# Hedgehog attention and a squared-ReLU FFN on one core: 24 output stores issued from GpSimd's queue in place of SyncE's

## The chip, the core and the metric

The kernel runs on one core of a Trainium2 chip. A core has a matrix engine (TensorE, PE in the profile), a vector engine (VectorE, DVE), a scalar engine (ScalarE, ACT), a general engine (GpSimd, POOL) and a synchronization engine (SyncE, SP), which here only issues DMAs. Each engine runs its own stream of instructions in order; they meet at semaphores. DMAs are issued by SP, ACT and POOL, and 16 DMA engines move the bytes. The metric is device time in microseconds (us); less is better.

## The reference

```python
def phi(x):
    proj = np.einsum('bhsd,df->bhsf', x, w_phi)
    proj = proj - np.max(np.abs(proj), axis=-1, keepdims=True)
    return np.concatenate([np.exp(proj), np.exp(-proj)], axis=-1)
q_p, k_p = (phi(q), phi(k))
kv = np.einsum('bhsf,bhsd->bhfd', k_p, v)
z = np.sum(k_p, axis=2)
num = np.einsum('bhsf,bhfd->bhsd', q_p, kv)
den = np.einsum('bhsf,bhf->bhs', q_p, z)[..., None] + 1e-06
attn = num / den
x = attn.transpose(0, 2, 1, 3).reshape(B * S, H * D)
h = np.maximum(x @ w_in, 0.0)
out = h * h @ w_out
```

Sizes: 8 batches, 8 heads, 576 tokens, head size 64, 128 features (256 with both signs); then 4608 tokens of 512 values through a layer of 2048. Inputs and the output are 32-bit floats in the chip's main memory (HBM). The kernel computes in bf16 with sums in 32 bits.

## The kernel before

**Attention.** For each batch the kernel loads k, q and v (L249, L257, L269; batch 0 and 1 also L278) with DMAs issued by GpSimd, which turn the floats into bf16 on the way. There are two buffers for each of k, q and v (`xk`, `xq`, `xv`), so batch b + 2 goes where batch b was. From batch 2 on, k and q are turned by DMA transposes issued by SP into `kT` and `qT` (L331); TensorE projects them with `w_phi` (L347), VectorE takes the maxima of their absolute values (L405, L498, L531), and ScalarE makes the exponentials. `va` (L428) is v, scaled; TensorE sums k's features times `va` into `kv` (L462). For batches 3 to 7 q's features are made with tokens in the partitions (`qf`, L544) and turned by another DMA transpose on SP into `qpn` (L548). TensorE then multiplies `qpn` with `kv` (L648), VectorE divides (L660 to L674) into `xo`, and a third kind of DMA transpose on SP (L708) turns `xo` into `xT`, which the FFN takes. The last 64 tokens of each batch are gathered in `xS`.

**FFN.** Its tokens come in 9 chunks of 512: chunk c is the first 512 tokens of batch c, and chunk 8 is all that is gathered in `xS`. The first product is `ffn_in` (L788, 64 matmuls of 512 columns a chunk); ScalarE or VectorE takes the ReLU out of PSUM into `hr` (L765, L767), VectorE squares it into `h` (L774). The second is `ffn_out` (L882): four output tiles of 128 tokens by 512 values a chunk. ScalarE or VectorE copies each tile out of PSUM to one of four buffers `ot` (`copy`, L193 and L195), and a DMA stores it to `out` (L900; 256 KB). Chunk 8 stores halves (L897), and its last tile pieces of these (L869). An `ot` buffer is written again four tiles later, and its store must have landed by then.

**The order of work.** The function does not emit instructions straight away. It adds operations to a plan (`Plan.add`), and at the end emits them in a written-out list, `ORDER`, of some 1,680 operation numbers; the attention of one batch is thereby laced with the FFN of the batches before. `pin` chains each instruction behind the one that its engine got before, so every engine, and the DMA queue of every engine, goes through its share of `ORDER` in that order. An instruction that waits holds everything behind it on its engine. `BASES` gives the PSUM banks, `STATES` picks ScalarE or VectorE for the copies that either could do, and `GATES` names, for each load of batches 2 to 7, one more operation that it must wait for. These lists are constants. The engine name and the cost that `add` is given matter to whoever made the lists; for an operation without an alternative they change nothing that is emitted. What decides who issues a DMA is the call inside `fn` (`nc.sync` or `nc.gpsimd`).

So SP's queue holds, in order, the transposes of L331, L548 and L708 and the stores of L900 and L897, and POOL's queue holds the loads. A DMA also waits on its queue for the semaphore that it will raise to be free: each kind of queue has eight, used in turn, so a DMA is issued when the one eight before it has landed.

Of the kernel before, what the change touches and what calls it, by code (L numbers as in the profile page):

```python
# [20 lines left out]
def act_cost(n):  # L21
    return max(n / 1200 + 0.050, 0.105), n / 1200 + 0.165 + SEM


def dve_cost(n):
    return n / 960 + 0.064, n / 960 + 0.150 + SEM


def pe_cost(n, each):
    return n * each, n * each + 0.165 + SEM  # L30
# [23 lines left out]
class Plan:  # L54
# [6 lines left out]
    def add(self, eng, cost, fn, r=(), w=(), opens=None, closes=None, dma=None, tiled=False, release=False, what="", lock=None):  # L61
        op = Op(eng, cost, fn, opens, closes, dma, tiled, release, len(self.ops), what)
        op.lock = lock
        before = {}

        def after(o, wait):
            before[o] = max(before.get(o, 0.0), wait)

        for t in r:
            o = self.writer.get(t)  # L70
            if o is not None:
                after(o, 0.0 if o.eng == eng == "PE" else 1.0)
        for t in w:
            o = self.writer.get(t)
            if o is not None:
                after(o, 0.0 if o.eng == eng else 1.0)
            for o in self.readers.get(t, ()):
                after(o, 0.0 if o.eng == eng else 1.0)
        for t in r:
            self.readers.setdefault(t, []).append(op)  # L80
        for t in w:
            self.writer[t] = op
            self.readers[t] = []
        before.pop(op, None)
        for o, wait in before.items():
            o.succ[op] = wait
        op.n = len(before)
        self.ops.append(op)
        self.banks.extend(op.opens)
        return op  # L90
# [18 lines left out]
def kernel(  # L109
# [10 lines left out]
    nc = tc.nc  # L120
# [12 lines left out]
    def dep(i, before, kind):  # L133
        tc.add_manual_dep(i, before, mybir.DependencyInfo(kind, mybir.DependencyReason.DATA), reason="order")

    def pin(ins):
        i = ins.ins
        before = last_on.get(i.engine)
        if before is not None:
            dep(i, before, mybir.DependencyClass.NoSync)  # L140
        last_on[i.engine] = i.name
        if now[0].seq in GATES:
            dep(i, plan.ops[GATES[now[0].seq]].ins, mybir.DependencyClass.Sync)
        now[0].ins = i.name
        return ins
# [8 lines left out]
    def ring(name, n, shape, dt=BF16):  # L154
        return [sb(f"{name}{i}", shape, dt) for i in range(n)]
# [27 lines left out]
    ot = ring("ot", NOT, [DM], F32)  # L183
    SL = (B * S // P - 1) % NOT
# [3 lines left out]
    add = plan.add  # L188

    def copy(out, in_):  # L190

        if now[0].eng == "DVE":
            pin(nc.vector.tensor_copy(out=out, in_=in_))  # L193
        else:
            pin(nc.scalar.activation(out=out, in_=in_, func=ACT.Copy))  # L195

    def ps1(g):
        return psum[:, g.base, :]
# [556 lines left out]
                    out_ops(c)  # L755


    hslot = [0]

    def relu_sq(g, dst, toks):  # L760
# [112 lines left out]
    def ffn_out(c, tt, part):  # L873
        if (c, tt) == (NCH - 1, 3):
            last_out(c, tt, part)
            return
        if part == 0:
            opb[c, tt] = Bank(1, "op")
        g = opb[c, tt]
        def fn():  # L880
            for mc in range(4 * part, 4 * part + 4):
                pin(nc.tensor.matmul(out=ps1(g), lhsT=h2[c % 2][mc // 4][:, mc % 4, tt * P : (tt + 1) * P],  # L882
                                     rhs=wout[mc // 4][:, mc % 4, :], start=(mc == 0), stop=(mc == MC - 1)))
        add("PE", pe_cost(4, 0.216), fn, r=[("wout", part)] + [("h2", c % 2, 4 * part + i, tt) for i in range(4)],
            w=[g], opens=g if part == 0 else None, what="F2")
        if part == 3:
            sl = oslot[0] % NOT
            oslot[0] += 1
            def fn():
                copy(ot[sl], ps1(g))  # L890
            o = add("ACT", act_cost(512), fn, r=[g], w=[("ot", sl)], closes=g, what="ot")
            plan.either((o, "DVE", dve_cost(512)))
            for u in range(2 if c == NCH - 1 else 1):
                def fn(u=u):
                    if c == NCH - 1:
                        b = 2 * tt + u
                        pin(nc.sync.dma_start(out=out[b * S + 512 : b * S + 576, :], in_=ot[sl][u * 64 : u * 64 + 64, :]))  # L897
                    else:
                        o = out[c * S : c * S + 512, :].rearrange("(p j) n -> j p n", j=4)[tt]
                        pin(nc.sync.dma_start(out=o, in_=ot[sl]))  # L900
                add("SP", (0.5, 0), fn, r=[("ot", sl)] + [("ot", SL, half) for half in range(2) if sl == SL],
                    dma=(0.37 if c == NCH - 1 else 0.74, HW_IN, "st"), what="st")


    for hi in range(2):
        def f_kcast(hi=hi):
            copy(xk[0][:, 256 * hi : 256 * hi + 256], ot[2][:, 256 * hi : 256 * hi + 256])
        o = add("DVE", dve_cost(256), f_kcast, r=[("xkf", hi)], w=[("xkh", hi)], what="kcast")
# [21 lines left out]
    for c in range(NCH + 1):  # L930
        if c + 1 < B:
            b = c + 1
            if b >= 2:
                load(k, xk, b, "xk", prs=PIECES, release=True)
                load_q(b, release=True, prs=PIECES)
                load(v, xv, b, "xv", prs=PIECES, release=True)
            attention(b)
        for i in range(16):
            if c == 0:
                if i < 4:  # L940
                    ffn_in_halves(c, 0, i)
                elif i < 8:
                    ffn_in_small(c, 1, i % 4)
                else:
                    ffn_in_pair(c, i - 8)
            elif c < NCH:
                ffn_in(c, i)
            if c >= 1:
                ffn_out(c - 1, i // 4, i % 4)
# [158 lines left out]
```

## Time and profile before

| | |
|---|---|
| median of 3 runs | 344.13 us (344.02 to 344.96) |
| profiled execution, first to last instruction (its span; no other time of it is known) | 344.8 us |
| granted TensorE clock, mean | 0.998 |
| busy: PE, DVE, ACT, POOL | 335.5, 264.2, 225.4, 95.5 us |
| stores of 256 KB by SP | 32, median 2.9 us from issue to landing |
| loads and other DMAs by POOL | 138 instructions |
| moved by DMAs | 51.51 MB, 149 GB/s mean |

A row of the groups reads: line, engine, operation, what it writes and reads, shape, count, then the time that the group was busy, the mean of one, and the engine's idle time just before them with what ended it. PE's busy time counts pipelined matmuls; a matmul of 512 columns shows 0.38 us while four in a row take 0.86 us. The issue of a DMA takes time on the engine's queue (SPq, or POOL itself), its landing comes later. In the timeline rows the first number is the start in us from the start of the span, the second the time that the row covers; several alike are merged with a count (x2). The chain of work that ended last is followed back from the end, and its DMA entries are stretches in which the next step stood waiting for a transfer.

### The profile page before, as it was taken

The page shows a single profiled execution, that of the slowest core. Times are in us where ns is not written, and L with a number is a line of the kernel's source. Part 1 is how long each engine was busy: PE and PEld are TensorE (multiplying, and loading weights), DVE is VectorE, ACT ScalarE, POOL GpSimd, SP SyncE. Part 2 cuts the span into 40 slices and gives each one's busy share as a digit, 9 for nine tenths or more (in the row PEclk, how much of TensorE's full clock was granted, in tenths as well). Part 3 has the DMA queues.
Part 4 walks back from the last instruction along what each step waited for, and adds up shares of the span by engine and source line. Part 5 has one row for each costly group of instructions (what it writes and reads, how often), then busy time and mean ns, then how long its engine had stood idle before and what let it go on. Part 6 is the DMA issues. An engine that isn't in the chain of part 4 may idle for free.

```text
span 344.8 us, 8417 instructions
## 1 busy us (share of the span) xinstructions
PE 335.5 (97%) x3389; PEld 188.3 (55%) x3389; DVE 264.2 (77%) x485; ACT 225.4 (65%) x393; POOL 95.5 (28%) x143
## 2 busy tenths in 40 slices
PE   8999999799999999999999999999999999999995
PEld 7679776444654555545545554565555444444443
DVE  4999999699877987788898999687876635757510
ACT  4999996489898898476887797798475503210031
POOL 8670671681730390104604051240000000000000
PEclk9999999999999999999999999999999999999999
DMA  9999999999999999999999999999864821101024
GB/s 139 179 206 202 199 132 157 153 118 205 170 175 172 227 165 185 195 182 183 171 207 172 199 164 195 188 154 168 196 125 96 157 62 38 63 0 61 32 68 115
DMA packets 142935, 51.51 MB, mean 149 GB/s; under 512 B 111472, under 2 KB 138416, under 8 KB 142896
## 3 DMA queue, kind: packets, MB, share of 16 engines
q1 hardware_dynamic: 97488, 32.35, 50.7%
q0 software_dynamic: 44960, 18.23, 46.7%
q8 instruction: 26, 0.43, 0.5%
q10 hardware_dynamic: 448, 0.39, 0.4%
q14 instruction: 13, 0.11, 0.1%
HBM read 36.73 MB, written 9.44 MB: 134 GB/s over the span
## 4 chain that ended last, share of the span: by engine, by line
PE 87%; DMA 6%; DVE 3%; ACT 1%; POOL 1%; issue 0%; POOLq 0%; DVEq 0%; SPq 0%
PE psum L788 32%; PE psum L882 31%; PE psum L648 5%; PE psum L462 5%; PE psum L347 5%; DMA xT<-xo 4%; DMA qpn<-qf 3%; PE psum L827 2%; PE psum L569 1%; DVE mk L405 1%; PE psum L813 1%; PE psum L799 1%; PE psum L846 1%; PE psum L450 1%; PE psum L320 1%; PE psum L961 1%
## 5 line engine op out<-in xcount | busy, mean ns | idle before, releaser
L882 PE MATMUL psum<-wout,h 128*128 128x512 bf16 x560 | 132.6, 380 | 0.0
L788 PE MATMUL psum<-xT,win 128*128 128x512 bf16 x448 | 106.1, 379 | 0.6 <-DMA xT<-xo 0.6
L765 ACT ACTIVATE hr<-psum 128x512 bf16<-128x512 f32 x98 | 57.1, 600 | 57.7 <-PE psum L788 50.2
L882 PEld LDWEIGHTS <-h 128*128 128x128 bf16 x560 | 51.1, 98 | 56.5 <-issue 0.3
L788 PEld LDWEIGHTS <-win 128*128 128x128 bf16 x512 | 46.7, 97 | 51.9 <-DMA xT<-xo 1.4
L774 DVE TENSOR_TENSOR h<-hr 128x512 bf16<-128x512 bf16 x144 | 56.0, 415 | 18.7 <-ACT hr L765 18.2
L544 ACT ACTIVATE qf<-psum 128x1024 bf16<-128x1024 f32 (+1 forms) x50 | 46.1, 939 | 5.5 <-PE psum L347 2.0
L405 DVE TENSOR_REDUCE mk<-psum 128x8 f32<-128x1024 f32 (+1 forms) x38 | 42.4, 1120 | 3.9 <-PE psum L347 2.0
L411 ACT ACTIVATE kn<-psum 128x1024 bf16<-128x1024 f32 (+1 forms) x38 | 35.7, 948 | 8.2 <-PE psum L347 4.7
L411 ACT ACTIVATE kp<-psum 128x1024 bf16<-128x1024 f32 (+1 forms) x38 | 35.8, 951 | 4.8 <-PE psum L347 4.0
L648 PEld LDWEIGHTS <-qpn 128*128 128x128 bf16 x624 | 27.5, 97 | 16.6 <-issue 3.1
L767 DVE TENSOR_SCALAR hr<-psum 128x512 bf16<-128x512 f32 x46 | 31.1, 684 | 5.7 <-PE psum L788 4.2
L660 DVE TENSOR_TENSOR psum<-psum,en 128x520 f32<-128x520 f32 (+1 forms) x39 | 27.2, 702 | 10.3 <-PE psum L648 6.1
L648 PE MATMUL psum<-kv,qpn 128*128 128x65 bf16 x624 | 30.6, 193 | 2.5 <-DVE xo L674 2.4
L269 POOL DMA_DIRECT2D xq<-in_q_dram x24 | 17.3, 727 | 55.2 <-DVE h L774 14.3
L531 DVE TENSOR_REDUCE mq<-psum 128x8 f32<-128x1024 f32 (+1 forms) x25 | 27.8, 1112 | 3.3 <-PE psum L347 2.5
L674 DVE TENSOR_TENSOR xo<-psum,rden 128x512 bf16<-128x512 f32 (+1 forms) x39 | 26.4, 684 | 3.7 <-DMA xT<-xo 3.2
L249 POOL DMA_DIRECT2D xk<-in_k_dram x27 | 20.0, 744 | 32.5 <-ACT en L508 16.0
L584 ACT ACTIVATE qpn<-psum 128x1024 bf16<-128x1024 f32 (+1 forms) x30 | 26.8, 955 | 2.5 <-PE psum L569 2.2
L195 ACT ACTIVATE ot<-psum 128x512 f32<-128x512 f32 x24 | 14.4, 598 | 20.3 <-PE psum L882 20.1
L428 DVE TENSOR_TENSOR va<-xv,va 128x1280 bf16<-128x1280 bf16 (+2 forms) x34 | 23.4, 714 | 0.8 <-ACT va L420 0.8
L249 POOL DMA_DIRECT2D xv<-in_v_dram x27 | 19.9, 744 | 14.7 <-PE psum L788 11.1
(79 smaller groups left out, 348.9 us busy)
## 6 DMA issues: line engine op xcount, KB each, us to landing
out_dram<-ot SPq DMA_DIRECT2D x32, 256.0 KB, 2.9
xk<-in_k_dram POOLq DMA_DIRECT2D x25, 128.0 KB, 5.6
xq<-in_q_dram POOLq DMA_DIRECT2D x24, 128.0 KB, 4.5
xv<-in_v_dram POOLq DMA_DIRECT2D x24, 128.0 KB, 5.0
win<-in_moe_w_in_dram POOLq DMA_DIRECT2D x4, 512.0 KB, 9.8
wout<-in_moe_w_out_dram POOLq DMA_DIRECT2D x4, 512.0 KB, 15.1
xq<-in_q_dram POOLq DMA_DIRECT2D x4, 256.0 KB, 6.4
out_dram<-ot SPq DMA_DIRECT2D x6, 128.0 KB, 2.3
```

The costliest lines, as they stand in the source:

```text
L249: pin(nc.gpsimd.dma_start(out=x[:, m0 + a * 512 : m0 + z * 512].rearrange("p (h x) -> p h x", x=4 * D), in_=src[b][2 * a : 2 * z, 0:512, : ...
L405: pin(nc.vector.tensor_reduce(out=mk_view(g), in_=ps2(pj)[:, :, : n * Fd].rearrange("p e (i f) -> p e i f", f=Fd), axis=AX.X, op=ALU.max, ...
L411: pin(nc.scalar.activation(out=dst[slot][:, :, :n, :].rearrange("p e i f -> p e (i f)"), in_=ps2(pj)[:, :, : n * Fd], func=ACT.Exp, scale= ...
L531: pin(nc.vector.tensor_reduce(out=mqb[:, c, :, :n], in_=ps2(pj)[:, :, : n * Fd].rearrange("p e (i f) -> p e i f", f=Fd), axis=AX.X, op=ALU ...
L544: pin(nc.scalar.activation(out=o, in_=i_, func=ACT.Exp, scale=sgn))
L648: pin(nc.tensor.matmul(out=o[:, u // 4, u % 4 * D1 : (u % 4 + 1) * D1], lhsT=qpn[slot][:, sg * half + u * m : sg * half + u * m + P], rhs= ...
L660: pin(nc.vector.tensor_tensor(out=o, in0=o, in1=enb[:m, c, :].rearrange("t (b h) -> t b h", b=2).to_broadcast([m, 2, 4, D1]), op=ALU.mult))
L765: pin(nc.scalar.activation(out=hr[sl], in_=ps1(g), func=ACT.Relu))
L767: pin(nc.vector.tensor_scalar(out=hr[sl], in0=ps1(g), scalar1=0.0, scalar2=None, op0=ALU.max))
L774: pin(nc.vector.tensor_tensor(out=dst, in0=i_, in1=i_, op=ALU.mult))
L788: pin(nc.tensor.matmul(out=o, lhsT=win[mc // 4][:, kc, mc % 4 * P : (mc % 4 + 1) * P], rhs=x, start=(kc == 0), stop=(kc == KC - 1)))
L882: pin(nc.tensor.matmul(out=ps1(g), lhsT=h2[c % 2][mc // 4][:, mc % 4, tt * P : (tt + 1) * P], rhs=wout[mc // 4][:, mc % 4, :], start=(mc = ...
```

## The change

The output tiles of chunks 1 to 6 are stored by DMAs that GpSimd issues on its own queue. The stores of chunks 0, 7 and 8 stay with SP. `ORDER`, `GATES`, `BASES` and `STATES` are the same, so the 24 stores take the places among POOL's loads that `ORDER` gives them, and SP goes through the rest without them. One line is added ahead, so lines from 758 on have numbers one higher in the changed kernel (L900 is L901, L882 is L883).

```diff
+    SWDGE = range(1, 7)
     hslot = [0]
...
                         o = out[c * S : c * S + 512, :].rearrange("(p j) n -> j p n", j=4)[tt]
-                        pin(nc.sync.dma_start(out=o, in_=ot[sl]))
-                add("SP", (0.5, 0), fn, r=[("ot", sl)] + [("ot", SL, half) for half in range(2) if sl == SL],
+                        pin((nc.gpsimd if c in SWDGE else nc.sync).dma_start(out=o, in_=ot[sl]))
+                add("POOL" if c in SWDGE else "SP", (0.5, 0), fn, r=[("ot", sl)] + [("ot", SL, half) for half in range(2) if sl == SL],
                     dma=(0.37 if c == NCH - 1 else 0.74, HW_IN, "st"), what="st")
```

In the order of POOL's queue the 24 stand like this: two behind the load that the profile of before shows at 102.99 us, two behind that of 128.52, two behind that of 139.12, one behind that of 155.80, one behind that of 167.37, two behind that of 186.09, three behind that of 207.57, and eleven behind the last load, that of 231.00.

## The prediction

> **What bounds the kernel now.** I read the page first: the busy shares, the DMA slices and the chain that ended last.
>
> ```profile
> PE 335.5 (97%) x3389; PEld 188.3 (55%) x3389; DVE 264.2 (77%) x485; ACT 225.4 (65%) x393; POOL 95.5 (28%) x143
> DMA  9999999999999999999999999999864821101024
> PE 87%; DMA 6%; DVE 3%; ACT 1%; POOL 1%; issue 0%; POOLq 0%; DVEq 0%; SPq 0%
> out_dram<-ot SPq DMA_DIRECT2D x32, 256.0 KB, 2.9
> ```
>
> TensorE carries 87% of the chain, and DMAs 6%. The DMA engines are busy in nine tenths or more of every slice up to about 265 us: bytes that are moved in time meet other bytes there. The last row counts the stores of whole tiles: 32, four for each of chunks 0 to 7, so 24 move and 8 stay.
>
> Next, where TensorE idles. The table by stretches starts at 66 us, because SP issues its first store only at 81 us and everything ahead of it is the same in both kernels. Columns: length, busy time of PE, granted clock, DMA share, GB/s.
>
> ```profile
> 66.00:110.00 44.00, 43.98 (x454) 1.00 1.28 163
> 110.00:111.00 1.00, 0.42 (x3) 1.00 0.54 198
> 111.00:137.00 26.00, 26.00 (x264) 1.00 1.31 200
> 137.00:138.00 1.00, 0.87 (x20) 1.00 1.69 43
> 138.00:270.00 132.00, 132.00 (x1345) 1.00 1.07 174
> ```
>
> In 204 us TensorE idles 0.58 + 0.13 + 0.02 = 0.73 us, at two places. The waits from 103 us on name both (PE the matmuls, PEld the weight loads), and the chain shows the transfers that ended last:
>
> ```profile
> PE psum L788 <- DMA xT<-xo: 0.6, 1, 0.6
> PEld L788 <- DMA xT<-xo: 1.4, 2, 1.1
> PEld L648 <- DMA qpn<-qf: 0.6, 1, 0.6
> ...
> 104.10 6.58 DMA xT<-xo
> 127.71 9.62 DMA qpn<-qf
> ```
>
> Both are SP's transposing DMAs. So a gain has at most 0.73 us to take, while a transfer that lands later at one of these two places is paid in full.
>
> **The change part by part.** SP loses 24 store issues, POOL gains them at the places that the written order gives.
>
> ```profile
> L900 SPq DMA_DIRECT2D out_dram<-ot x32: 332/570/1302, 81.2 to 334.4; - x32
> DMA to landing us min/median/max: 2.2/2.9/6.3
> ...
> 102.67 1.33 SPq L548 DMA_TRANSPOSE qpn<-qf  x1
> 104.10 3.31 SPq L708 DMA_TRANSPOSE xT<-xo  x2
> 107.46 0.57 SPq L900 DMA_DIRECT2D out_dram<-ot  x1
> ...
> 111.59 0.57 SPq L900 DMA_DIRECT2D out_dram<-ot  x1
> ```
>
> *SP.* It is freed of 24 x 0.57 = 13.7 us of issuing. The stores of chunk 0 stay (the fourth is the one at 107.46); the first that leaves is the one at 111.59. The xT transposes that TensorE waits for are issued at 104.10 and just after, ahead of it, so this relief cannot reach the 0.58 us wait. It can reach the 0.13 us one. Behind that, SP's transposes come some 0.6 us earlier per store, and since TensorE waits for none of them, that is worth nothing. Bounds: -0.13 to 0; I take 0.
>
> *POOL, the first pair of stores.* In the new order the first two stores follow the load that POOL issues at 102.99, with nothing else to wait for, because ScalarE had written both ot tiles:
>
> ```profile
> 102.99 0.71 POOL L269 DMA_DIRECT2D xq<-in_q_dram  x1 [5.21 <-PE psum L648]
> 118.05 1.40 POOL L269 DMA_DIRECT2D xq<-in_q_dram  x2 [14.35 <-DVE h L774]
> ...
> 99.82 0.59 ACT L195 ACTIVATE ot<-psum 128x512 f32<-128x512 f32 x1
> ...
> 101.33 0.59 ACT L195 ACTIVATE ot<-psum 128x512 f32<-128x512 f32 x1
> ```
>
> They go out at about 103.7 and 104.4 instead of at 111.59 and behind it, that is, inside the flight of the xT transposes (104.10 to 110.68). How fast such a transfer gets to the engines, and how full these are:
>
> ```profile
> L269 POOL DMA_DIRECT2D xq<-in_q_dram x24: 698/717/771, 39.8 to 230.3; - x24
> ...
> DMA to landing us min/median/max: 3.1/4.5/6.9
> ...
> 100.00:104.00 4.00, 4.00 (x52) 2.18 (x50) 3.34 (x5) 4.00 (x9) 0.71 (x1) 1.00 1.26 198
> 104.00:111.00 7.00, 6.42 (x70) 3.04 (x66) 6.11 (x9) 6.12 (x11) 0.00 (x0) 1.00 1.18 165
> ```
>
> POOL's issue of such a load takes 0.72 us and lands 4.5 us after it began; stores begun at 103.7 and 104.4 would land around 108 to 109, so their bytes move between about 105 and 109, beside the xT bytes. Two stores are 2 x 262 KB = 524 KB. No row shows a store on POOL's queue, so I bound it. Above: all of it goes ahead of xT, at the 198 GB/s of the stretch before, 524/198 = 2.6 us. Below: the stores' bytes wait for xT's, 0. (A gain at this place is excluded, for xT is issued first.) I take the middle, 1.3 us, because the queues alternate in the rows: the load of 102.99 moved while SP's transposes of 102.67 and 104.10 were under way. TensorE already waits for xT, so all of the delay is paid: +1.3.
>
> *The second pair.* SP's two at 132.16 go behind POOL's series of 16 loads that begins at 118.05 and ends so:
>
> ```profile
> 132.16 1.05 SPq L900 DMA_DIRECT2D out_dram<-ot  x2
> ...
> 128.52 0.65 POOL L257 DMA_DIRECT2D xk<-in_k_dram  x1
> 138.43 0.70 POOL L269 DMA_DIRECT2D xq<-in_q_dram  x1 [9.26 <-PE psum L347]
> ```
>
> They are issued at 129.2 and 129.9, while the critical qpn of 127.71 flies until 137.33. Above it is again 2.6 us; below -0.13, since on SP the same two stores were in flight beside it as well. They stand last in POOL's queue behind those 16, so I take 0; that cover is gone if the loads have drained early.
>
> *POOL's loads behind the other stores.* The other 20 stand as follows: two after the load of 139.12, one after that of 155.80, one after 167.37, two after 186.09, three after 207.57, eleven after the last load. Each pushes the loads behind it by 0.72 us, unless POOL then waits anyway. It does in all places but two:
>
> ```profile
> 155.80 0.70 POOL L249 DMA_DIRECT2D xk<-in_k_dram  x1 [15.97 <-ACT en L508]
> 156.49 0.71 POOL L249 DMA_DIRECT2D xv<-in_v_dram  x1
> ...
> 169.87 1.49 POOL L249 DMA_DIRECT2D xv<-in_v_dram  x2
> 182.49 0.71 POOL L269 DMA_DIRECT2D xq<-in_q_dram  x1 [11.14 <-ACT hr L765]
> ...
> 156.63 1.40 SPq L900 DMA_DIRECT2D out_dram<-ot  x2
> ```
>
> The five loads from 156.49 and the five from 167.97 on go out 0.7 us later, and their bytes follow 262 KB more, at 198 GB/s another 1.3 us. The last xv load of 170.6, which lands about 7 us later by its row below, feeds the va products at 178.2 to 179.5:
>
> ```profile
> L249 POOL DMA_DIRECT2D xv<-in_v_dram x2: 776/780/784, 169.9 to 170.6; - x2
> DMA to landing us min/median/max: 7.2/7.2/7.2
> L428 DVE TENSOR_TENSOR va<-xv,va x3: 683/821/821, 178.2 to 179.5; 128x1280 bf16<-128x1280 bf16 x2, 128x1024 bf16<-128x1024 bf16 x1
> ```
>
> 170.6 + 7.2 = 177.8, some 1 us of cover. Bounds 0 to +1.0 (0.7 + 1.3 less 1.0), and I take 0, because two stores leave SP's queue in the same stretch (156.63), which frees the engines as much. A store that waits for its tile could hold loads too; only stores with no near load behind them do.
>
> *Sum.* 0 + 1.3 + 0 + 0 = +1.3 us on the profiled 344.8 us, which is 0.7 us above the median of the runs (344.13). On the median: 345.4 us.
>
> [...]
>
> **The rivals.**
> - *Nothing measurable.* The store bytes fall into gaps, xT lands as before: 344.0 to 344.6, say 344.3. For it: a store on SP landed in 2.2 us at best, and the moved bytes are the same. Against it: the DMA row of nines. [...]
> - *Not slower: SP's relief wins.* The place is SP's queue behind 111.59. It decides if the first pair does not delay xT and the qpn of 127.71 lands 0.13 us or more earlier. Price: -0.13, and at the very most both waits, -0.73: 343.4 to 344.0. Against it: only two waits are left to remove.
> - *Loads become the bound.* At 155 to 180 us the loads behind a store land late and VectorE waits for xv: +1.0 at each of two places on top of 1.3, so +3.3: 347.4. For it: a DMA share above 1.
> - *POOL's issues wait for VectorE.* A store's issue that had to sit out one of VectorE's longest operations,
>
> ```profile
> L405 DVE TENSOR_REDUCE mk<-psum 128x8 f32<-128x1024 f32 (+1 forms) x38 | 42.4, 1120 | 3.9 <-PE psum L347 2.0
> ```
>
> would cost 1.1 us more, at the two places with loads close behind 2.2 us, on top of 1.3: +3.5, 347.6. Against it: the row of L269, longest issue 0.77. [...]
> - *The move does not free ot sooner.* If stores sit behind gated loads, ScalarE or VectorE wait for an ot tile. Against it: by the rows above all but the last few go out earlier than on SP. Price below 1 us, with TensorE covered: within the first rival.
>
> **How the numbers follow.** Delay of xT 0.52 (its own range 344.5, little delay, to 346.8, the whole 2.6); nothing 0.28; relief 0.08; loads 0.09; slowed issue 0.03. The likeliest gives 345.4. About 0.3% (1.03 us) is what a measurement of this kernel can tell from no change, so slower starts at 345.16. Of the first case 0.40 lies above that and 0.12 below it; slower 0.40 + 0.09 + 0.03 = 0.52; faster, under 343.10, gets 0.07, though by these rows the relief ends at 343.4, for causes that no row names; same 0.41. Range: from 343.6, which leaves out most of the relief, to 347.4, which holds the xT bound and reaches to the loads' case.
>
> **What would show it.** POOL's timeline with stores at about 103.7 and 104.4 and issues near 0.7 us; the chain's "DMA xT<-xo" of 6.58 grown by about 1.3, and TensorE's idle time in the microsecond after 110 grown with it; the wait for qpn at 137 not longer; SP's transposes from 111 on 0.6 us or more earlier, with no effect on TensorE; no wait of va for xv. It is wrong if xT lands no later (stores too late or engines not the limit), if the two waits vanish, or if a new wait of VectorE or TensorE for a load or an ot tile shows up after 150 us.

## The result, and the profile after

The changed kernel takes 349.18 us (median of 4 runs, 347.95 to 351.7) against 344.07 us before: 1.0131 times as long, 95% interval 1.009 to 1.0171. A second comparison, with 6 and 23 runs, gave 348.47 against 344.35 us, ratio 1.0122 (1.01 to 1.0144). The change costs some 4.2 to 4.5 us. The prediction had said 345.4 us and a range up to 347.4; the sign was right, the size was not.

The page of the changed kernel: busy times, the share of the chain by engine, the group of the moved stores, the two busiest queues, and the moved stores' DMAs.

```profile
PE 335.0 (97%) x3359; PEld 188.2 (54%) x3389; DVE 264.6 (76%) x485; ACT 225.3 (65%) x393; POOL 109.0 (31%) x167
PE 87%; DMA 6%; DVE 3%; ACT 2%; issue 1%; POOL 1%; POOLq 0%; ACTq 0%; DVEq 0%
L901 POOL DMA_DIRECT2D out_dram<-ot x24 | 13.4, 561 | 80.0 <-ACT ot L195 57.5
q0 software_dynamic: 46880, 24.52, 52.4%
q1 hardware_dynamic: 94032, 26.06, 43.3%
out_dram<-ot POOLq DMA_DIRECT2D x24, 256.0 KB, 4.9
out_dram<-ot SPq DMA_DIRECT2D x8, 256.0 KB, 3.2
```

POOL's 24 issues take 0.56 us each, less than the 0.72 of its loads, and nothing waits for them: POOL is no bound. But a moved store lands 4.9 us after its issue (median), one of the eight that stayed with SP 3.2. TensorE's share of the chain is 87% as before, so the loss is not one engine's work but time lost at single places.

The waits from 100 to 165 us (engine, line, what it waited for: us in all, times, longest), and then the chain of the same stretch (start, us, what):

```profile
PEld L789 <- DMA xT<-xo: 3.4, 2, 3.1
PE psum L789 <- DMA xT<-xo: 2.6, 1, 2.6
```

```profile
101.41 8.75 DMA xT<-xo
110.21 6.18 PE psum L789 x20
146.96 6.41 DMA qpn<-qf
```

PE's wait for xT, 0.6 us before, is now 2.6, and xT took 8.75 us in place of 6.58. The wait for qpn at 137 us is gone from this list, because TensorE comes there later; a new step, qpn at 146.96, has come instead. The first two stores in POOL's timeline, 0.8 us behind the issue of the first xT transpose at 101.41; in the kernel before, the first store of this pair went out 7.5 us behind it (111.59 and 104.10):

```profile
102.25 1.12 POOL L901 DMA_DIRECT2D out_dram<-ot  x2 [1.11 <-ACT en L514]
```

And the table by stretches (length, PE busy, granted clock, DMA share, GB/s):

```profile
107.00:110.00 3.00, 0.57 (x3) 1.00 1.02 83
110.00:112.00 2.00, 1.79 (x5) 0.61 1.23 294
112.00:114.00 2.00, 2.00 (x6) 0.53 1.18 238
```

TensorE idles 2.43 us of the three ahead of 110, and then works at 0.61 and 0.53 of its clock: 20 matmuls take 6.18 us in the chain where 4.51 stood before.

One thing in xT's step is not the stores' doing. In the kernel before, in slices of 0.3 us from 100 us on:

```profile
GB/s 189 138 83 67 155 257 235 289 290 291 290 283 18 203 203 150 203 189 157 116 175 255 226 202 214 266 252 172 83 57 102 0 8 9 14 375 375 185 240 288
```

From 109.3 to 110.5 us the DMA engines move nothing but 31 packets of SP's queue, all but one of them under 512 bytes, and xT lands at 110.68, just behind that. Ahead of it, from some 108.5 us on, one packet of 16 KB of an instruction queue had been under way, the one packet of this row (DMAs of the kernel before from 108.4 to 110.4 us):

```profile
q8 instruction: 1, 0.02, 3.4%
```

3.4% of 16 engines' 2 us is 1.1 us on one engine. In eight profiles whose chain holds this xT step (the two of this section, and from the experiments the first pair alone, early on SP and on ScalarE's queue, chunk 6 alone, and the second profiles of the changed kernel and of the fill), a stretch of 0.6 to 1.5 us at 26 GB/s or less ends 0.2 to 0.9 us ahead of the landing, by slices of 0.3 us, and one such packet moves between 100 and 112 us; after the change the stretch is from some 108.5 to 109.9 us, and the packet was under way from 107.67 to 109.09. So a part of xT's step is not a sharing of the engines with the stores. Whether xT's last bytes wait for that packet no run tests; the stretch is there with and without the moved stores, so it does not explain the difference.

Two warnings on this pair of profiles. The span after (346.6 us, an execution of 348.65) is compared with a span of 344.8 before, and that execution of before had lost some 2.3 us at 63 us, ahead of any moved store (TensorE idles 2.37 us from 60 to 66 us, 0.12 in the changed kernel, and 0.05 to 0.86 with the first pair alone, all but the first pair, all 24 with the pair later, and the fill); so the loss is larger than 346.6 less 344.8. (A span is 1.7 to 2.2 us shorter than the time of the same execution wherever both are known here, so by an estimate that execution of before took some 346.5 to 347 us; the prediction held its span against the times of other executions, but added its terms to their median.) And what one profiled execution shows need not be what the median pays, as the experiments make plain.

### The profile page after: what moved, and what is told of

Read it like the earlier page. It is cut to its first block, busy times and chain, and to the rows that moved or that the text cites. A ratio compares the mean times of both kernels' runs of the same rounds, so it can differ in the third digit from the quotient of the medians.

```text
span 346.6 us, 8394 instructions
## 1 busy us (share of the span) xinstructions
PE 335.0 (97%) x3359; PEld 188.2 (54%) x3389; DVE 264.6 (76%) x485; ACT 225.3 (65%) x393; POOL 109.0 (31%) x167
## 3 DMA queue, kind: packets, MB, share of 16 engines
q0 software_dynamic: 46880, 24.52, 52.4%
q1 hardware_dynamic: 94032, 26.06, 43.3%
## 4 chain that ended last, share of the span: by engine, by line
PE 87%; DMA 6%; DVE 3%; ACT 2%; issue 1%; POOL 1%; POOLq 0%; ACTq 0%; DVEq 0%
PE psum L883 33%; PE psum L789 30%; PE psum L648 5%; PE psum L347 5%; PE psum L462 5%; DMA xT<-xo 4%; PE psum L828 2%; DMA qpn<-qf 2%; PE psum L569 1%; PE psum L814 1%; PE psum L800 1%; PE psum L847 1%; PE psum L320 1%; ACT qf L544 1%; PE psum L450 1%
## 5 line engine op out<-in xcount | busy, mean ns | idle before, releaser
L883 PE MATMUL psum<-wout,h 128*128 128x512 bf16 x530 | 128.5, 379 | 2.0 <-issue 0.6
L789 PE MATMUL psum<-xT,win 128*128 128x512 bf16 x448 | 108.2, 383 | 3.1 <-DMA xT<-xo 2.6
L883 PEld LDWEIGHTS <-h 128*128 128x128 bf16 x560 | 51.1, 97 | 56.6 <-issue 0.3
L901 POOL DMA_DIRECT2D out_dram<-ot x24 | 13.4, 561 | 80.0 <-ACT ot L195 57.5
```

The source lines that it names most:

```text
L789: pin(nc.tensor.matmul(out=o, lhsT=win[mc // 4][:, kc, mc % 4 * P : (mc % 4 + 1) * P], rhs=x, start=(kc == 0), stop=(kc == KC - 1)))
```

## The experiments

Theory A, from the two traces: the first pair of stores delays xT (2.05 us more idle time at that place) and the long idle lowers the clock (6.18 less 4.51, 1.67 us). Rival B: each of the 24 moved stores takes its share. Times are medians; "+" is the ratio's distance from 1, as a share of 344.3 us.

**First pair alone, and all but the first pair.**

```diff
-    SWDGE = range(1, 7)
+    SWDGE = ((1, 3), (1, 0))
...
-                        pin((nc.gpsimd if c in SWDGE else nc.sync).dma_start(out=o, in_=ot[sl]))
+                        pin((nc.gpsimd if (c, tt) in SWDGE else nc.sync).dma_start(out=o, in_=ot[sl]))
```

The complement has in `SWDGE` all (c, tt) of chunks 1 to 6 without (1, 3) and (1, 0).

> Only the first two stores of chunk 1 (output tiles 3 and 0, the pair that GpSimd issued at 102.25 us) go from GpSimd; the other 22 stay with SyncE. Theory A (this pair takes the DMA engines from the transposes of xT that TensorE waits for, 8.75 us in the chain of waits in place of 6.58, and the granted TensorE clock falls to 0.61 and 0.53 right behind the long idle, 6.18 us in the chain for 20 waits in place of 4.51): 2.05 + 1.67 = 3.7 us over the kernel before, 347.4 to 348.6 us, with the stall at 107 to 110 us and the low clock in the profile. Rival B (the sum of all 24 moved stores makes the loss, through GpSimd's queue and smaller effects all over): 344.0 to 345 us, since 2 of 24 are left.

> The complement: 22 stores go from GpSimd, and the first two stores of chunk 1 stay with SyncE. Theory A: the stall at the xT transposes and the low clock are gone; what is left is +0.93 us at 153 to 156 us and -0.49 us at 137 us of the comparison of the traces, so 344.0 to 345.2 us. Rival B: nearly the whole loss stays, 348 to 349.5 us.

Measured: the pair alone 346.21 us against 344.34, ratio 1.005 (1.003 to 1.007), +1.7 us; the other 22 alone 345.96 us, 1.0048 (1.0029 to 1.0067), +1.7 us. Both theories miss: the pair costs much for 2 stores of 24 and not the whole, and the 22 cost as much again (1.7 + 1.7 = 3.4 us, somewhat less than all 24, inside the intervals). The chain of the kernel with the pair alone, then that of the kernel with the other 22:

```profile
101.79 8.07 DMA xT<-xo
```

```profile
101.68 6.73 DMA xT<-xo
125.44 11.21 DMA qpn<-qf
```

The pair lengthens xT to 8.07 us. Without the pair xT takes 6.73, as before, but now qpn takes 11.21 us where it took 9.62. These transposes of qpn are in flight when the second pair of chunk 1 goes out.

**The first pair two loads later.** Numbers 736 and 682 of `ORDER` are moved behind 937.

```diff
-    ..., 698, ..., 736, 669, ..., 682, ..., 935, ..., 937, ..., 931, ...
+    ..., 698, ..., 669, ..., 935, ..., 937, 736, 682, ..., 931, ...
```

> All 24 stores go from GpSimd, but the first two stand two loads later in its order, behind the loads that the changed kernel issued at 117.75 us, when the xT transposes have long landed. Theory A (it is the time of the pair, not the queue it is on): as in the run with 22 stores, 344.0 to 345.5 us. Rival C (stores from GpSimd's queue cost this much wherever they stand, being served in another way than those of SyncE): 348 to 349.5 us.

> Only the first pair goes from GpSimd, two loads later (near 118 us, where the run with all 24 had it too). Theory E (a store costs what it delays, and nothing critical is in flight at 118 us; SyncE, freed of two issues, sends qpn earlier, which took 0.51 us off the wait at 137 us in the run with the first pair alone): 343.7 to 344.4 us. Rival C (a store from GpSimd's queue costs something wherever it stands): as with the first pair at 102 us, 346 us.

Measured: all 24 with the pair later 347.99 us, 1.0103 (1.0071 to 1.0134), +3.5 us; only the pair, later, 345.25 us, 1.0023 (1.0005 to 1.0041), +0.8 us. Both expectations of a recovery were wrong; rival C, a price wherever the store stands, had 348 and 346 us, the first of which was met, and the stores of chunk 6, below, speak against it. With all 24, the chain has these DMA steps:

```profile
103.11 5.96 DMA xT<-xo
126.10 10.76 DMA qpn<-qf
145.51 6.04 DMA qpn<-qf
```

xT is whole again (5.96), and qpn pays instead. With the pair alone, POOL's timeline, and then the chain's step:

```profile
117.21 1.13 POOL L901 DMA_DIRECT2D out_dram<-ot  x2
118.31 0.75 POOL L249 DMA_DIRECT2D xk<-in_k_dram  x1
```

```profile
125.48 10.38 DMA qpn<-qf
```

The pair goes ahead of most of the loads of that series, and these go out later by its 1.13 us. The stores had landed 5.0 and 5.4 us after their issue, at some 122 and 123 us, ahead of the qpn of 125.48, so qpn (10.38) did not meet their bytes; it met loads that were later. So a store may also cost through the loads that it pushes. That rests on this one profile, in which TensorE waited 1.0 us for xT as well.

**The second pair alone, chunks 2 to 6 alone, chunk 6 alone.** `SWDGE` is ((1, 2), (1, 1)), then all of chunks 2 to 6, then all of chunk 6.

> Only the second pair of chunk 1 (its output tiles 2 and 1) goes from GpSimd. Theory E: the wait for qpn at 137 us grows by some 1.6 us, 345.6 to 346.2 us. Rival B: 2 of 24 stores, 344.3 to 344.9 us.

> The 20 stores of chunks 2 to 6 go from GpSimd, all four of chunk 1 stay with SyncE. Theory E (two pairs of chunk 1 each delay a transposed transfer that TensorE waits for: the first pair xT at 110 us, +1.48 us in the run with that pair alone; the second pair qpn at 137 us, +1.59 us in the run without the first pair, where qpn took 11.21 us from 125.44 to 136.65; the other 20 cost little): 344.2 to 345.0 us. Rival B (each moved store has its share, 24 cost some 4.9 us): 20 cost 4.1 us, 348.4 us.

> Only the four stores of chunk 6 go from GpSimd. In the changed kernel they were issued from 287.61 to 300.27 us, where SyncE has one transpose left (293.03 us). Theory F (a store costs time by delaying a transpose that TensorE waits for): nothing, 344.1 to 344.7 us. Rival B (each of 24 has its share of 4.9 us): +0.8 us, 345.2 us.

| moved to GpSimd | median, us | ratio (95%) | us |
|---|---|---|---|
| first pair of chunk 1 | 346.21 | 1.005 (1.003 to 1.007) | +1.7 |
| second pair of chunk 1 | 345.43 | 1.0037 (1.0014 to 1.006) | +1.3 |
| the 20 of chunks 2 to 6 | 345.48 | 1.0027 (1.0011 to 1.0044) | +0.9 |
| of these, the 4 of chunk 6 | 344.55 | 1.0007 (0.9994 to 1.0021) | +0.2 |
| all 24, second comparison | 348.47 | 1.0122 (1.01 to 1.0144) | +4.2 |

1.7 + 1.3 + 0.9 = 3.9 us, which is the loss of all 24 within the intervals. So the loss adds up from three parts. An equal share per store (rival B) would give 0.35 us for a pair and 3.5 for the 20, which the rows exclude; theory E was near, with the 20 somewhat above what it allowed. The 22 together had measured +1.7, less than 1.3 + 0.9 but inside the intervals. The execution of the second pair that was profiled is the fastest of its twelve (344.63 us), and shows less of a stall than the kernel with the 22 stores, a wait of TensorE for qpn of 0.6 us:

```profile
125.07 10.05 DMA qpn<-qf
```

Chunk 6, whose stores go when SP has hardly a transpose left (in the changed kernel from 287.61 us on, with one transpose behind that, at 293.03), costs nothing that can be measured.

What two late stores do can be read cleanly, since at 250 us no loads are left. First the kernel with chunks 2 to 6 moved, its DMAs from 250 to 260 us (busy tenths and GB/s in 40 slices, then issues with the median us to landing) and, below them, the step of its chain; then the kernel with the second pair alone, its DMAs from 249 to 259 us:

```profile
DMA  9999999889989999999999995899969023000000
GB/s 209 224 215 218 221 181 168 229 302 331 219 142 168 168 135 222 125 150 146 201 136 109 218 128 42 191 203 102 213 132 119 13 100 134 0 0 0 0 0 0
out_dram<-ot POOLq DMA_DIRECT2D x2, 256.0 KB, 5.8
qpn<-qf SPq DMA_TRANSPOSE x2, 7.1
```

```profile
250.10 9.80 DMA qpn<-qf
```

```profile
DMA  9999999999999999996000000000030000000000
GB/s 217 207 214 215 221 218 206 151 181 259 218 211 215 221 215 218 206 196 155 0 0 0 0 0 0 0 0 0 0 66 0 0 0 0 0 0 0 0 0 0
qpn<-qf SPq DMA_TRANSPOSE x2, 4.6
```

Alone, the transposes move some 215 GB/s, and the engines fall silent 4.8 us into the stretch. With two stores of POOL's queue beside them the engines are busy for about 8 us, at rates that mostly lie between 100 and 220 GB/s: more bytes, and moved more slowly (by the slices shown 1.45 MB in 8.5 us, some 171 GB/s, against 0.99 MB in 4.75 us, some 207). The transpose issued at 250.10 lands after 9.80 us. In that execution (346.88 us, the slowest of ten) it held ScalarE and then TensorE. TensorE idles 1.64 us from 245 to 270 us, and 0.11 with the second pair alone. So when stores fall on such a transpose they can cost some 1.5 us, but they don't fall so in every execution. Where the 20 stores cost their +0.9 us in the other nine, no profile shows.

**Which stall, and the clock.** Idle matmuls fill part of the wait for xT, so that TensorE is not idle long; beside it the changed kernel itself a second time.

```diff
-    156: (7, 2), 101: (7, 2), 128: (7, 9), 134: (5, 4), 142: (5, 6),
+    156: (7, 2), 101: (7, 2), 128: (7, 9), 134: (5, 4), 142: (5, 6), 669: (7, 32),
```

> The changed kernel with 32 idle matmuls of 128x128 on the warm tile ahead of the first matmul that waits for xT of chunk 1, so that TensorE is idle for some 1.5 us less there; the wait for the transposes ends as before. Theory A (the clock is lowered by the length of the idle stretch of 3.2 us, and that costs 1.67 us): the granted clock stays at 1.00 at 110 to 114 us, and the time is some 1.7 us below the changed kernel's 349.18 us, 347 to 348 us. Rival D (the clock falls for another reason, or the slower matmuls are made up for later): 349 us, or the low clock is still there.

> The changed kernel as it is, once more, beside the same with idle matmuls: 348 to 350 us by the first comparison.

> The changed kernel with 32 idle matmuls ahead of the first matmul that waits for xT of chunk 1, once more, on the same chip as the changed kernel itself. Theory A (the fall of the clock is part of the loss in the median): 1 to 1.7 us below the changed kernel. Rival D (the clock falls in some executions only, or the time is made up for): within 0.7 us of it.

Measured: first comparison 348.29 us, ratio 1.013 (1.0081 to 1.0179); second 348.64 us, 1.0126 (1.0106 to 1.0145), beside the changed kernel's 348.47. The fill keeps the clock and saves nothing that these few runs can tell. The kernel with the fill, second time, by stretches, and its chain:

```profile
110.00:112.00 2.00, 1.82 (x9) 1.00 1.22 287
```

```profile
101.97 8.17 DMA xT<-xo
110.18 4.48 PE psum L789 x20
141.89 7.71 DMA qpn<-qf
155.18 7.51 DMA qpn<-qf
```

And the chain of the changed kernel, second time:

```profile
103.67 6.38 DMA xT<-xo
126.64 11.20 DMA qpn<-qf
```

Here the clock had not fallen at all, the stall at xT was milder, and the second pair's stall at qpn was there (11.20 us), which the first profile had not shown. So the fall of the clock, read from one profile, belongs to some executions only: the mean granted clock of the first four runs was 0.994, 1.0, 0.999 and 0.995, and the one at 1.0 took 347.95 us, still 3.9 us over before. Theory A's 1.67 us is not in the median (rival D); with four runs that spread over 1.4 us beside six that spread over 2.3, a smaller share is not excluded. The executions with a low mean clock are mostly among the slowest of their kernels: with the second pair alone two at 0.994 and 0.995 took 348.4 and 348.47 us, the other ten 344.63 to 346.58. Whether the low clock makes them slow or a long stall makes both, no run beside the fill parts.

**Why a store on another queue delays a transpose.** Early stores on SP's own queue: in the kernel before, 736 and 682 are moved between the two xT transposes, behind 455.

```diff
-    ..., 455, ..., 464, ..., 509, ..., 620, ..., 736, ..., 756, ..., 682, ...
+    ..., 455, 736, 682, ..., 464, ..., 509, ..., 620, ..., 756, ...
```

> The kernel before, all stores with SyncE, but the first pair of chunk 1 stands earlier in its order, between the two xT transposes that TensorE waits for at 110 us. Theory F (any 512 KB in flight beside these transposes delays them, whichever queue sends them): at least what the first pair alone cost from GpSimd, 346.2 us, and up to two issues of 0.57 us more, 347.3 us. Rival G (it is how GpSimd's queue cuts a store, 64 packets of 4096 bytes where SyncE's has 128 of 2048, that starves the transposes): only the issues count, 344.3 to 345.5 us.

The opposite: the kernel before, without the load that flies beside xT. Its `ORDER` has 745, that load, and 756, the transpose qT of what it brings, right ahead of 935.

```diff
-    745: 459, 746: 396,
+    745: 669, 746: 396,
```

> The kernel before with the other traffic beside the xT transposes taken away: the load that GpSimd issued at 102.99 us (128 KB) waits for the first matmul that uses xT (L788), and the transpose of what it loads (qT, first used at 132 us) stands behind the xS transpose in SyncE's order; all stores with SyncE. Theory F (any transfer in flight beside these transposes delays them): xT takes some 4.4 us, as it did in quieter places, in place of 6.58, the wait of 1.17 us at 110 us shrinks, 343.3 to 344.0 us. Rival H (only stores hurt, loads do not, or the transposes are slowed by each other): 344.2 to 344.8 us.

And the stores on a third queue, ScalarE's: the first pair (`(c, tt)` in ((1, 3), (1, 0)), with 736 and 682 behind 618 in `ORDER`), and all 24 where they stand.

```diff
-                        pin((nc.gpsimd if c in SWDGE else nc.sync).dma_start(out=o, in_=ot[sl]))
+                        pin((nc.scalar if c in SWDGE else nc.sync).dma_start(out=o, in_=ot[sl]))
```

> The first pair of chunk 1 is issued by ScalarE on its own queue at about the time at which GpSimd issued it (102 to 104 us); all other stores with SyncE. ScalarE loses its time for two issues (0.42 us each for a DMA of its own at the start, 0.67 at the end). Theory J (bytes on any queue other than that of the transposes slow the transposes that are already in flight): xT takes some 8 us, as with GpSimd (8.07 us), where it took 5.07 us with the two stores behind it on SyncE's own queue; 346 to 347 us. Theory G (GpSimd's way of cutting a store, 4096 bytes a packet, does it): xT takes 5 to 6.6 us, and the time is 344.4 to 345.5 us, what there is being ScalarE's two issues.

> All 24 stores of chunks 1 to 6 are issued by ScalarE, at the same places of the order; it loses 24 issues of 0.42 to 0.67 us, 10 to 16 us of its idle time of some 120 us, part of which delays TensorE. Theory J: the loss of the changed kernel, 4.1 us, is there again, 348.4 us or more. Theory G: 344.4 to 346.5 us, and the transposes' flights are those of the kernel before.

Measured: early on SP 345.5 us, 1.0036 (1.0019 to 1.0052), +1.2 us; load later 344.82 us, 1.0017 (0.9986 to 1.0049), with eleven runs from 343.1 to 348.13 (a twelfth, 350.01, is left out of both); first pair from ScalarE 347.17 us, 1.0063 (1.0039 to 1.0087), +2.2 us; all 24 from ScalarE 347.68 us, 1.0091 (1.007 to 1.0111), +3.1 us, less than theory J's 348.4 (there the first store went out at 108.3 us, behind the xT transposes). The xT transposes' rows from 100 to 112 us, last column the median us of the two to landing: the kernel before, the one with the load later, the one with early stores on SP (and SP's timeline and the chain's step), the one with the pair on ScalarE (and its chain's step), and the changed kernel.

```profile
xT<-xo SPq DMA_TRANSPOSE x2, 5.8
```

```profile
xT<-xo SPq DMA_TRANSPOSE x2, 4.0
```

```profile
xT<-xo SPq DMA_TRANSPOSE x2, 5.0
```

```profile
101.17 1.94 SPq L708 DMA_TRANSPOSE xT<-xo  x1
103.20 1.08 SPq L900 DMA_DIRECT2D out_dram<-ot  x2
104.38 1.22 SPq L708 DMA_TRANSPOSE xT<-xo  x1
```

```profile
104.38 4.93 DMA xT<-xo
```

```profile
xT<-xo SPq DMA_TRANSPOSE x2, 6.1
```

```profile
102.47 7.25 DMA xT<-xo
```

```profile
xT<-xo SPq DMA_TRANSPOSE x2, 7.8
```

Without the load xT takes 4.0 us where it took 5.8, as theory F has it for loads too. But the time is rival H's, not theory F's 343.3 to 344.0 us, and the nearly idle stretch ahead of xT's landing is missing in that profile as well, so what shortened xT is not parted.

Early on SP's own queue each xT transpose flies only 5.0 us, but that is no sign of less delay: the two stores stand between the two transposes and push the second one's issue. From the issue of the first transpose at 101.17 to the last landing at 104.38 + 4.93 = 109.31 it is 8.1 us. The same stretch is 6.4 to 6.7 us in kernels that leave this pair where it was (chunk 6 alone, all but the first pair), 7.25 with ScalarE's queue, and 8.07 and 8.75 with GpSimd's. TensorE's wait for xT goes the same way: 0.4 us in those kernels (0.6 in the one before), 1.2 with the early stores on SP, 1.3 with ScalarE's, 2.1 and 2.6 with GpSimd's. And the losses of the pair on the three queues, +1.2 (0.7 to 1.8), +2.2 (1.3 to 3.0) and +1.7 us (1.0 to 2.4), overlap. So theory J, that the bytes must be on a queue of their own, is not shown: what the three kernels have in common is that 512 KB go out between the two xT transposes or beside them, which is theory F (though the time on SP is below the 346.2 us that it named), and the move to GpSimd matters because it makes the stores go out at that time. GpSimd's cutting of a store is different, as the queues' rows of the kernel before show beside those of the changed one:

```profile
q1 hardware_dynamic: 97488, 32.35, 50.7%
q0 software_dynamic: 44960, 18.23, 46.7%
```

The 24 stores took q1 97488 - 94032 = 3456 packets, 144 each, and take q0 46880 - 44960 = 1920, 80 each. But the loss is there with ScalarE's queue as well. How much of ScalarE's +2.2 us is its own time for two issues the runs do not separate, and the +1.2 us on SP lie at the edge of rival G's range, so whether the packets add something stays open.

The load that was moved away from xT came back elsewhere. The kernel with the load later, its DMAs from 114 to 130 us and its chain:

```profile
xv<-in_v_dram POOLq DMA_DIRECT2D x4, 128.0 KB, 8.6
qT<-xq SPq DMA_TRANSPOSE x1, 11.4
```

```profile
125.36 12.21 DMA qpn<-qf
```

qT, now beside the series of loads, took 11.4 us, the loads 8.6, and qpn 12.21 us: what was won at 110 us was lost at 137 in this execution (346.87 us), and the spread of its runs shows that it goes either way. No kernel here beats the one before.

## Why the prediction was wrong

**What bounds the kernel: right.** The reading that the engines are full (but for the nearly idle stretch ahead of xT's landing), that TensorE waits only for SP's transposes, and that a later landing at those two places is paid in full, is what the chains above show between 100 and 165 us. What it missed is that transposes which had cover in one profile (the qpn's at 147, 155 and 250 us) are as open to delay, and that their cover is small.

**SP's relief: right.** It brought nothing; no variant became faster.

**POOL, the first pair: the mechanism right, the size low.** The stores went out at 102.25 and just after (predicted 103.7 and 104.4, each in its own profile) and xT's step grew from 6.58 to 8.75 us. The term was +1.3 with bounds 0 to 2.6; the pair alone measured +1.7 (1.0 to 2.4). Not all of xT's step is bytes that compete, as the nearly idle stretch ahead of its landing shows, so that the middle of the bounds came out near is in part luck.

**The second pair: this step failed.** The term was 0, because the two stores stand last in POOL's queue behind 16 loads. Measured +1.3 (0.5 to 2.1), which lies inside the bound of 2.6 that the step gave and then did not use. The step took the place behind 16 loads for cover. It was none: in the kernel with the 22 stores the pair went out at 127.56 and behind it, while the last of these loads was in flight (issued at 126.94, landed after 6.5 us, at 133.4), and the stores landed at some 134.1 and 136.6 us, beside the qpn that TensorE waited for, which landed at 136.65 after 11.21 us where it took 9.62. The prediction had named one way to lose the cover, loads that have drained early; that was not the way.

**POOL's loads behind the other stores: this step failed too.** It looked for delayed loads and a wait of va for xv, found 1 us of cover, and put 0. No such wait appeared. The 20 stores cost +0.9 (0.4 to 1.5) by another way. The one profile of them, of their slowest execution, shows two of them falling on a transpose of SP's that had cover before (the qpn of 250.10); for the rest of the 20 the place of the cost stays open. The argument that the engines lose as many bytes on SP's queue as they get on POOL's leaves out the time: the same bytes go out earlier or later, and what is in flight then pays.

So of 4.2 us, 1.3 were in the sum. Missing were 0.4 of the first term, two terms set to 0 on the strength of cover seen in one execution (1.3 and 0.9), and 0.3 that the three parts, measured alone, leave open within their intervals. The fall of the clock, which was not in the prediction, is in the profile; in the median a fill that kept the clock up changed nothing.

**The rivals.** Nothing measurable, SP's relief, and ot not freed sooner: no. Loads as the bound and slowed issues had the times nearest to the result, 347.4 and 347.6, by waits that did not come. The trace of the changed kernel shows no issue of POOL's that VectorE lengthens: the 24 took 0.54 to 0.61 us each beside a VectorE busy 76%, and where POOL stood idle ahead of one until VectorE was done (21.4 us, four times), it was VectorE's copy into the ot tile that the store waited for. The 1.1 us a place of that rival is an estimate from the length of VectorE's operations alone. For "nothing measurable" the prediction had that the moved bytes are the same; they are, but they went out at other times, at +1.2%.

## What to carry to other kernels

The stores moved to another engine's queue went out at another time (the first pair at 102.25 us in place of 111.59), and shared the DMA engines with what was in flight then: before moving a DMA, list which transfers are in flight at its new time and who waits for each, those with a little cover included. Where the engines are full (here nine tenths busy or more up to some 265 us), do not set a term to zero because one profiled execution shows cover; price it by the time that its bytes take (2.6 us for a pair by the prediction's bound, where +1.7 and +1.3 us were measured), and expect another execution to stall somewhere else (here at 110 us, or at 110 less and at 137). Where a profile shows a striking loss (here the clock), test it alone before it goes into the account.

## What the hardware showed that was not expected

- At 250 us a lone pair of 256 KB stores beside transposes kept the engines busy for some 8 us at some 171 GB/s, where the transposes alone ran at some 207 GB/s: the mixture moved less per us than the transposes alone.
- Ahead of the landing of the xT that TensorE waits for, the engines move 0 to 14 GB/s for 1.2 us in the kernel before (109.3 to 110.5 us); a 16 KB packet of an instruction queue, which took 1.1 us of one engine, was under way ahead of that stretch.
- Behind a wait of 3.1 us of TensorE's weight loads (2.6 of its matmuls) the granted clock was 0.61 and 0.53 for some 4 us; behind one of 2.6 us (2.1 of its matmuls) it stayed at 1.00. The second is the kernel with the first pair alone, its wait and then its clock:

```profile
PEld L789 <- DMA xT<-xo: 2.9, 2, 2.6
```

```profile
110.00:112.00 2.00, 2.00 (x10) 1.00 1.26 274
```

Whether the length of the wait decides it no run shows, and why only some executions show the fall stays open.

- The same kernel stalled at different transposes in its two profiles (110 us, or 110 less and 137), at nearly the same total time.
